# Reordering one block's up items and two sets of weight sums in a fused attention and FFN kernel

## The chip, the cores and the metric

The kernel runs on one core of one Trainium2 chip. The metric is the device time of one execution in microseconds (us), the median of several runs. The core has five engines with a queue of instructions each: TensorE (PE in the profile, PEld for its weight loads), VectorE (DVE), ScalarE (ACT), GpSimd (POOL) and SyncE (SP), which here issues most of the transfers. Each engine works through its own queue in order and waits where an operand or a buffer is not ready; the queues wait for each other by semaphores.

## The reference

```python
q_n = q / (np.linalg.norm(q, axis=-1, keepdims=True) + 1e-06)      # k_n, c_n alike
q_assign = np.argmax(np.einsum('bhsd,hcd->bhsc', q_n, c_n), axis=-1)   # k_assign alike
mask = q_assign[:, :, :, None] == k_assign[:, :, None, :]
scores = scale * np.matmul(q, k.transpose(0, 1, 3, 2))
scores = np.where(mask, scores, -1000000000.0)
...
attn = attn / (np.sum(attn, axis=-1, keepdims=True) + 1e-09)
...
x = np.ascontiguousarray(attn_out.transpose(0, 2, 1, 3)).reshape(B * S, H * D)
h = x @ w_in
relu6 = np.clip(h + 3.0, 0.0, 6.0)
g = h * relu6 / 6.0
return (g @ w_out).astype(np.float32)
```

Four batches of 768 tokens, 8 heads of 64: attention in which a query sees only keys of its own cluster (16 per head), then a feed-forward block of 512 to 2048 to 512 with hard-swish. Inputs are 64-bit floats; the kernel works in 32 bits.

## The kernel before

The work has three stages. A **loop** (`for n in range(0, total + lag_d + 2, 2)`, "round n" below) does attention for the first two batches: 8 pairs of heads, 12 steps a pair, two steps a round. Each round issues the scores and exponentials of its steps (L400, L423), GpSimd's running sums over the exponentials (L430, L433, `acc`), and the products with the values of the two steps before (`pv`, L443). Every sixth step the sums are added up on TensorE (`pd`, L467), inverted and multiplied on VectorE (`rcp` L473, `num` L474) and written to `xd`. Between these stands the preparation of the next pair, by the place r of the round in the pair: transposes of queries and keys (`pqk`, L320) at r = 0 and 2, cluster scores (`pcs`, L337) at r = 4, their transposes and one-hot rows on VectorE (`pr`, `mx` L351, `one_hot` L357) at r = 6, and the transposes of the one-hot rows (`po`, L379; copied by ScalarE to `xm`, L384) at r = 8 and 10.

The same loop decodes the weights from 64 bits, in 32 chunks of five steps, mostly on VectorE (L232 to L259), a number of steps a round set by `share`. Behind the chunks, `decode` holds eight weight sums (L523): halves of T1, T2, T4 and T3, differences of the four blocks of `w_out`, 128 x 1024 each.

From round 60 on the loop also takes items of the feed-forward block of the first batch. An **up item** (L597, 16 matmuls into one PSUM bank `ph`) multiplies 256 tokens by two slices of `w_in`; ScalarE lifts the result (L499), VectorE clips it (L502), and after every second item GpSimd makes four sums of gated values (L635). The eight up items of this first block are multiplied out plainly; all later blocks use `halved` (L645, `uX`, `uY`), a seven-product scheme that needs, for each slice i, three sums of blocks of `w_in` (t1, t2, t4) and a fourth that replaces block b12 in place. `make_first_sums(i)` makes them (L556) and stores the three in DRAM (`td`, L557), from where later blocks load them (`tx`, L548); the sums for i = 0 and 1 stay in SBUF for the second block. As b12 is overwritten, the fourth sum of slice i can come only after the first block's up item i.

Behind the up items stand seven **down parts** of the block (L684), each in two halves, which multiply the gated values by `w_out` or T1 to T4 into the banks `X` and `Y`; VectorE and ScalarE take the banks into `y` (L691, L735). The first block's parts run at the end of the loop and in the second stage. Part 3 reads T3, which takes the place of one block of `w_out`, parts 0 and 1 read T2, part 2 T1, part 6 T4. In the first block each part's `end` also calls `make_first_sums` for the slices listed for it, ahead of its own `y` sums.

In the loop nearly all PSUM results of one bank (`ph`, `pqk`, `pcs`, `pr`, `pd`, `po`, `X`, `Y`) share two banks (`psum_m`, `scratch`), so each waits until the one before the last is read.

The second stage (`late_plan`) does attention for the other two batches over tokens sorted by cluster, with GpSimd scattering rows through DRAM (L1014, from the positions `pos`), mixed with feed-forward items; the third finishes the feed-forward block.

The order of all queues is the order in which the program issues (`manual_schedule`). Before, `want` spreads the items evenly from round 60 on, and places each ahead of the preparation of the same round; the list is 60, 64, 70, 74, 80, 84, 90, 94 for the up items and 100 for the first down part. `share` leaves weight sum 0 to round 90, 1 to 3 to round 92 and 4 to 7 to round 94.

Of the kernel before, what the change touches and what calls it, by code (L numbers as in the profile page):

```python
# [119 lines left out]
def fast_path(ctx, tc, ok, q, k, v, centroids, moe_w_in, moe_w_out, out):  # L120
# [390 lines left out]
    def weight_sums(i):  # L511
        if i == 0:
            decoding.close()
            wtp = pool("wtp", 1)
            for name in ("T1", "T2", "T4"):
                st[name] = wtp.tile([P, HF, HC], F32, name=name)
            st["T3"] = wb[0][1]
        name, a, b = (
            ("T1", wb[0][1], wb[0][0]), ("T2", wb[1][1], st["T1"]), ("T4", wb[1][0], st.get("T2")),
            ("T3", wb[1][1], wb[0][1]),  # L520
        )[i // 2]
        h = slice(i % 2 * HF // 2, (i % 2 + 1) * HF // 2)
        nc.vector.tensor_tensor(out=st[name][:, h], in0=a[:, h], in1=b[:, h], op=ALU.subtract)  # L523
# [15 lines left out]
    def wi(s, t, i):  # L539
        f = t * HF + i  # L540
        return w_in_sb[:, s * HK : (s + 1) * HK, f * P : (f + 1) * P]
# [5 lines left out]
            tx = st["tx", u] = txp.tile([P, 3, HK, P], F32, name="tx")  # L547
            nc.sync.dma_start(tx, td[:, i])  # L548

    def make_first_sums(i):  # L550

        tx = txp.tile([P, 3, HK, P], F32, name="tx")
        t1, t2, t4 = (tx[:, k] for k in range(3))
        b11, b12, b21, b22 = wi(0, 0, i), wi(0, 1, i), wi(1, 0, i), wi(1, 1, i)
        for out_, in0, in1 in ((t1, b12, b11), (t2, b22, t1), (t4, b21, t2), (b12, b22, b12)):
            nc.vector.tensor_tensor(out=out_, in0=in0, in1=in1, op=ALU.subtract)  # L556
        nc.sync.dma_start(td[:, i], tx)  # L557
        if i < 2:
            st["tx", HF + i] = tx

    def token_sums(b, m):

# [15 lines left out]
    def ffn_items(b):  # L578
# [114 lines left out]
        def down(m, part):  # L693
            def keep(chunk, half, y, queue=nc.sync):
                queue.dma_start(out_v[b, 2 * m + chunk][:, half * HC : (half + 1) * HC], y)

            def multiply(second):
                if part < 2:
                    h = range(part * HF // 2, (part + 1) * HF // 2)
                    if second:  # L700
                        product(st["X"], 1, 5, st["T2"], False, True, False, h)
                    else:
                        product(st["X"], 0, 0, wb[0][0], True, False, False, h)
                    return
                kind, bank, half, w = (
                    (4, "Y", 0, st["T1"]), (1, "Y", 1, st["T3"]),
                    (2, "X", 0, wb[1][0]), (6, "Y", 0, wb[1][1]), (3, "Y", 1, st["T4"]),
                )[part - 2]
                h = range(second * HF // 2, (second + 1) * HF // 2)
                product(st[bank], half, kind, w, part == 2, part in (3, 4, 6), part > 3, h)  # L710

            def begin():
                raise_gates()
                if part == 0:
                    st["X"] = psum_m.tile([P, DM], F32, name="X", tag="m")
                    st["y0"] = yp.tile([P, DM], F32, name="y0", tag="y0")
                elif part == 2:
                    st["Y"] = st.get("psum_y", psum_m).tile([P, DM], F32, name="Y", tag="m")
                    st["y1"] = yp.tile([P, DM], F32, name="y1", tag="y1")
                multiply(0)  # L720

            def end():
                multiply(1)
                if part == 0:
                    finish()
                if (b, m, part) == (B - 1, NHC - 1, 6):
                    st["good"] = nc.values_load(ok[0:1, 0:1], min_val=0, max_val=1)
                if part == 4:
                    token_sums(*divmod(b * NHC + m + 1, NHC))
                if (b, m) == (0, 0):  # L730
                    for i in ([HF - 1, HF - 2], [5], [4], [], [3, 2], [0], [1])[part]:
                        make_first_sums(i)
                y0, y1 = st["y0"], st.get("y1")
                if part == 1:
                    nc.scalar.copy(out=y0[:, HC:], in_=st["X"][:, HC:])  # L735
                    add(y0[:, HC:], y0[:, HC:], st["X"][:, 0:HC])
                elif part == 3:
                    add(y1[:, 0:HC], y0[:, HC:], st["Y"][:, HC:])
                    add(y1[:, HC:], y1[:, 0:HC], st["Y"][:, 0:HC])
                    keep(1, 1, y1[:, HC:])  # L740
                elif part == 4:
                    nc.scalar.copy(out=y0[:, 0:HC], in_=st["X"][:, 0:HC])
                    keep(0, 0, y0[:, 0:HC])
                elif part == 6:
                    add(y1[:, 0:HC], y0[:, HC:], st["Y"][:, HC:])
                    keep(1, 0, y1[:, 0:HC])
                    add(y0[:, HC:], y0[:, HC:], st["Y"][:, 0:HC])

                    keep(0, 1, y0[:, HC:], nc.scalar if st["last"] else nc.sync)

            return [begin, end]

# [475 lines left out]
    per_batch = NKT * per_pair  # L1228
    total = FIRST * per_pair
    lag_v, lag_d = 2, 4  # L1230
    up_first = NFT // 2

    decode = [step for i in range(NW) for step in decoding_steps(i)]
    decode += [lambda i=i: weight_sums(i) for i in range(8)]
    READY, DECODED = per_batch + 2 * lag_d, 2 * per_batch

    def share(n, r):  # L1240


        if n < READY:
            return {0: 4, 2: 3, 4: 3, 6: 1, 8: 2, 10: 4}[r]
        if n < DECODED - per_pair:
            return {0: 6, 2: 5, 4: 4, 6: 3, 8: 5, 10: 5}[r]
        return {0: 6, 2: 5, 4: 4, 6: 1, 8: 3, 10: 4}[r]
# [2 lines left out]
    st["early"] = st["free"] = True  # L1250
    st["last"] = st["moving"] = False
    fill, checks = [], []
    st["done"] = 0

    def check_all():
        now, checks[:] = checks[:], []
# [7 lines left out]
    with tc.manual_schedule():  # L1264
        nc.scalar.dma_start(cen, centroids.rearrange("h c d -> (h c) d"))
        load(0, "q", "k")
        constants()
        load(0, "v")
        load_weights(0)
        centroid_norm()  # L1270
        for part in range(3):
            turn(0, part)
        idle(5)
        nc.vector.tensor_copy(out=ident_q, in_=ident)
        load(1, "q", "k")
        load_weights(1)
        cluster_scores(0)
        scores_qk(0)
        route(0)
        scores_qk(1)  # L1280
        for part in range(2):
            route_turn(0, part)

        for n in range(0, total + lag_d + 2, 2):
            g, r = divmod(n, per_pair)
            steps = [i for i in (n, n + 1) if i < total]
            prep = prep_items(g + 1, r)
            for i in steps:
                scores(i)
                exponentials(i)  # L1290
                key_sums(i)
            for i in (n - lag_v, n - lag_v + 1):
                if 0 <= i < total:
                    attn_v(i)
            m = n - lag_d + 1
            if m >= 0 and m % NCH == NCH - 1:
                later.append(divide(m))
                ready(m)
            if prep and r == 4:
                prep.pop(0)()  # L1300
            if r == 6:
                load(g + 2, "q", "k")
                load(g + 1, "v")
            want = min(max(n + 2 - READY, 0) * up_first // (DECODED - READY) - st["done"], len(fill) // 2)
            st["done"] += want
            for i in range(max(len(prep), want)):
                if i < want:
                    fill.pop(0)()
                    fill.pop(0)()
                if i < len(prep):  # L1310
                    prep[i]()
            if n < total:
                for step in decode[: share(n, r)]:
                    step()
                del decode[: share(n, r)]
            check_all()
            checks.extend(later)
            later.clear()

        while checks or later:  # L1320
            checks.extend(later)
            later.clear()
            check_all()
        st["early"] = False
        st["moving"] = True
        open_late()
        for i, point in enumerate(late_plan()):
            for op, *args in point:
                op(*args)
            busy = i >= AHEAD and (i - AHEAD) % SLOT in (6, 9)  # L1330
            if fill and not busy:
                fill.pop(0)()
        st["last"] = True
        st["moving"] = False
        flag = whether_good()
        while fill:
            fill.pop(0)()
            if len(fill) == HOLD:
                flag()
# [363 lines left out]
```

## Time and profile before

| | us |
|---|---|
| median of 3 runs | 957.33 (957.01 to 957.46) |
| the profiled execution | 959.56 |
| its span, first to last instruction | 957.8 |
| TensorE's granted clock | 0.998 |

The profile is one execution. Its page lists busy time by engine, the span in 40 slices, and groups of instructions by line, engine and operands. A row of the timeline has the start and the length in us, the engine, the line, the operation, and operands with shapes; "x16" means that so many instructions follow each other. In square brackets stands how long the engine stood idle before it, and what it then waited for. A row of waits has the sum, the number and the longest. A row of a stretch ("windows") has its bounds, its length, and the busy time of PE, PEld, DVE, ACT and POOL with the number of instructions, then TensorE's granted clock, the DMA engines' busy share and GB/s.

### The profile page before, as it was taken

To read this page: it belongs to the slowest core of one execution; us is meant where nothing else is said; L and a number is where in the kernel's file an instruction comes from. 1 tells how busy PE (TensorE), PEld (TensorE's weight loads), DVE (VectorE), ACT (ScalarE), POOL (GpSimd) and SP (SyncE) were. 2 spreads that over 40 slices of the span, in tenths; PEclk is the share of its full clock that TensorE was granted. 3 is DMA by queue.
4 is the path that set the end of the run, shared out by engine and by line. 5 is a ranking of instruction groups with operands and counts; after the bars stand their busy time and mean duration, and the time that the engine had idled before them with its cause. 6 is when DMAs were issued, how large, how long until landed. Compare 5 with 4: busy or idle time off the path is not lost.

```text
span 957.8 us, 17621 instructions
## 1 busy us (share of the span) xinstructions
PE 929.6 (97%) x6358; PEld 725.5 (76%) x6358; DVE 594.4 (62%) x1306; ACT 349.8 (37%) x731; POOL 576.3 (60%) x1302
## 2 busy tenths in 40 slices
PE   8999999999899999999999999999999999999997
PEld 5444445555698798787897988888888799999996
DVE  6789888989977276274483474374471564636261
ACT  6888877765112232222232231241331311202020
POOL 3877767657367577776777878767777160303030
PEclk9999999999999999999999999999999999999999
DMA  7255464350474557456584484654744333323210
GB/s 206 90 133 155 132 176 124 106 145 10 145 223 137 151 159 164 129 130 153 153 198 119 120 204 118 160 155 114 198 142 95 102 96 116 102 72 105 66 57 26
DMA packets 174351, 124.23 MB, mean 130 GB/s; under 512 B 134064, under 2 KB 152496, under 8 KB 174256
## 3 DMA queue, kind: packets, MB, share of 16 engines
q1 hardware_dynamic: 164320, 109.86, 42.7%
q0 software_dynamic: 9216, 12.60, 4.4%
q8 instruction: 52, 0.85, 0.4%
q10 hardware_dynamic: 720, 0.56, 0.2%
q14 instruction: 43, 0.35, 0.1%
HBM read 94.67 MB, written 28.31 MB: 128 GB/s over the span
## 4 chain that ended last, share of the span: by engine, by line
PE 67%; DVE 3%; DMA 2%; issue 1%; ACT 0%; SPq 0%; another core or an unknown queue 0%; ACTq 0%; DVEq 0%
PE Y L684 17%; PE uY L645 15%; PE X L684 12%; PE uX L645 11%; PE pv L1096 3%; PE ps L899 3%; PE ps L1057 3%; DMA piece<-qd 2%; PE pv L1057 1%; PE pd L1120 1%; PE pcs L337 1%; PE rk L981 1%; PE ps L1137 1%; DVE tx L556 0%; DVE w_out_sb L523 0%
## 5 line engine op out<-in xcount | busy, mean ns | idle before, releaser
L433 POOL TENSOR_TENSOR acc<-acc,ex 128x768 f32<-128x768 f32 x64 | 123.3, 1927 | 37.4 <-ACT ex L423 33.9
L1014 POOL DMA_INDIRECT qd<-qn,pos x96 | 96.2, 1002 | 54.8 <-issue 17.5
L1030 POOL DMA_INDIRECT xn<-xsd,pos x96 | 94.3, 982 | 46.0 <-ACT sx L499 24.3
L499 ACT ACTIVATE sx<-g_sb,half_c 128x512 f32<-128x512 f32 x88 | 63.8, 725 | 146.5 <-DVE g_sb L656 126.3
L635 POOL TENSOR_TENSOR g_sb<-g_sb 128x256 f32<-128x256 f32 x52 | 41.8, 825 | 122.1 <-DVE g_sb L502 121.1
L1014 POOL DMA_INDIRECT kvd<-kvn,pos x96 | 96.1, 1001 | 27.3 <-issue 25.4
L1006 POOL MEMSET w_low<- 128x1 f32 x864 | 91.3, 106 | 33.3
L691 DVE TENSOR_TENSOR y<-y,Y 128x256 f32<-128x256 f32 x48 | 20.2, 421 | 132.7 <-PE Y L684 131.9
L684 PE MATMUL X<-w_out_sb,g_sb 128*128 128x256 f32 x384 | 90.4, 382 | 4.0 <-DVE y L691 2.2
L645 PE MATMUL uX<-xb,w_in_sb 128*128 128x128 f32 x704 | 93.0, 275 | 0.0
L684 PE MATMUL Y<-T,g_sb 128*128 128x256 f32 x384 | 88.0, 381 | 0.0
L684 PE MATMUL Y<-w_out_sb,g_sb 128*128 128x256 f32 x384 | 87.7, 380 | 0.0
L645 PEld LDWEIGHTS uX<-xb,w_in_sb 128*128 128x128 f32 x704 | 85.7, 192 | 0.0
L684 PEld LDWEIGHTS X<-w_out_sb,g_sb 128*128 128x128 f32 x384 | 70.9, 190 | 18.5 <-issue 4.0
L684 PEld LDWEIGHTS Y<-T,g_sb 128*128 128x128 f32 x384 | 72.1, 190 | 13.2 <-issue 3.9
L684 PEld LDWEIGHTS Y<-w_out_sb,g_sb 128*128 128x128 f32 x384 | 71.9, 190 | 10.6 <-issue 1.3
L656 DVE TENSOR_TENSOR sx<-uX,sx 128x128 f32<-128x128 f32 x176 | 51.1, 290 | 45.9 <-ACT sx L663 30.8
L400 PE MATMUL ps<-xf 64*128 64x384 f32 x384 | 78.5, 487 | 0.6 <-ACT ex L423 0.6
L423 ACT ACTIVATE ex<-ps 128x768 f32<-128x768 f32 x96 | 72.6, 802 | 4.5 <-PE ps L400 4.5
L443 PE MATMUL pv<-ex,vt 128*64 128x384 f32 x384 | 72.5, 499 | 0.0
L502 DVE SCALAR_TENSOR_TENSOR g_sb<-sx,g_sb 128x512 f32<-128x512 f32 x88 | 63.9, 728 | 3.3 <-ACT sx L499 2.3
L656 DVE TENSOR_TENSOR g_sb<-uY,sx 128x128 f32<-128x128 f32 (+1 forms) x176 | 65.6, 414 | 0.0
(194 smaller groups left out, 1796.7 us busy)
## 6 DMA issues: line engine op xcount, KB each, us to landing
tx<-td SPq DMA_DIRECT2D x86, 384.0 KB
raw<-in_moe_w_in_dram SPq DMA_DIRECT2D x16, 512.0 KB
raw<-in_moe_w_out_dram SPq DMA_DIRECT2D x16, 512.0 KB
xb<-xd SPq DMA_DIRECT2D x12, 512.0 KB
out_dram<-y SPq DMA_DIRECT2D x44, 128.0 KB
qk<-in_q_dram SPq DMA_DIRECT2D x18, 192.0 KB
qk<-in_k_dram SPq DMA_DIRECT2D x18, 192.0 KB
vt<-in_v_dram SPq DMA_DIRECT2D x16, 192.0 KB
```

The costliest lines, as they stand in the source:

```text
L400: nc.tensor.matmul(st["ps", n][:, t, 0:HALF], lhsT=x[r, NCH + j], rhs=x[r, hf * NHC : (hf + 1) * NHC], start=first, stop=last, skip_group_ ...
L423: nc.scalar.activation(out=ex, in_=sc, func=ACT.Exp, scale=SM_SCALE)
L433: nc.gpsimd.tensor_tensor(out=acc, in0=acc, in1=ex, op=ALU.add)
L443: nc.tensor.matmul(pv[t * D : (t + 1) * D], lhsT=vt[:, t, j], rhs=ex[:, t], start=(j == 0), stop=(j == NCH - 1),)
L499: nc.scalar.activation(out=r, in_=h, func=ACT.Relu, bias=half_c, scale=1.0 / 6.0)
L502: nc.vector.scalar_tensor_tensor(out=g, in0=r, scalar=1.0, in1=h, op0=ALU.min, op1=ALU.mult)
L645: nc.tensor.matmul(dst, lhsT=w[:, kt], rhs=x(kt), start=(kt == 0), stop=(kt == HK - 1))
L656: nc.vector.tensor_tensor(out=out_, in0=in0, in1=in1, op=ALU.add)
L684: nc.tensor.matmul(bank[:, half * HC : (half + 1) * HC], lhsT=g_sb[:, kind, i], rhs=w[:, i], start=(first and i == 0), stop=(last and i == ...
L1006: nc.gpsimd.memset(w_low, W_LOW)
L1014: i = nc.gpsimd.indirect_dma_start(out=rows[name, g, t], in_=src, in_offset=None, out_offset=bass.IndirectOffsetOnAxis(ap=pos[:, a, j, t : ...
L1030: nc.gpsimd.indirect_dma_start(out=xn[:, j, t], out_offset=None, in_=rows["xsd", g, t], in_offset=bass.IndirectOffsetOnAxis(ap=pos[:, 0, j ...
```

## The change

The up items and the first down part get a list of rounds, `up_at`, and are taken after the preparation of the round. `make_first_sums` is split: `kept_sums(i)` makes t1, t2, t4 and stores them, the in-place subtraction remains. For the slices 7, 6, 5, 4 `kept_sums` runs in the loop at rounds 64, 70, 76 and 82, behind the decoding steps; for the others where it stood. The last four weight sums (T4 and T3) leave `decode` and are issued with down parts 0 to 3, T3 first. The sums of a down part now come after its `y` sums.

```diff
+    def subtract(out_, in0, in1):
+        nc.vector.tensor_tensor(out=out_, in0=in0, in1=in1, op=ALU.subtract)
+
+    def kept_sums(i):
         tx = txp.tile([P, 3, HK, P], F32, name="tx")
         t1, t2, t4 = (tx[:, k] for k in range(3))
-        b11, b12, b21, b22 = wi(0, 0, i), wi(0, 1, i), wi(1, 0, i), wi(1, 1, i)
-        for out_, in0, in1 in ((t1, b12, b11), (t2, b22, t1), (t4, b21, t2), (b12, b22, b12)):
-            nc.vector.tensor_tensor(out=out_, in0=in0, in1=in1, op=ALU.subtract)
+        for sums in ((t1, wi(0, 1, i), wi(0, 0, i)), (t2, wi(1, 1, i), t1), (t4, wi(1, 0, i), t2)):
+            subtract(*sums)
         nc.sync.dma_start(td[:, i], tx)
         if i < 2:
             st["tx", HF + i] = tx
+        st["kept"].add(i)
+
+    def make_first_sums(i):
+        if i not in st["kept"]:
+            kept_sums(i)
+        subtract(wi(0, 1, i), wi(1, 1, i), wi(0, 1, i))
...
                 if part == 4:
                     token_sums(*divmod(b * NHC + m + 1, NHC))
-                if (b, m) == (0, 0):
-                    for i in ([HF - 1, HF - 2], [5], [4], [], [3, 2], [0], [1])[part]:
-                        make_first_sums(i)
                 y0, y1 = st["y0"], st.get("y1")
...
                     keep(0, 1, y0[:, HC:], nc.scalar if st["last"] else nc.sync)
+                if (b, m) == (0, 0):
+                    for i in ([HF - 1, HF - 2], [5], [4], [], [3, 2], [0], [1])[part]:
+                        make_first_sums(i)
+                    if part in (0, 1):
+                        weight_sums(6 + part)
+                    elif part in (2, 3):
+                        weight_sums(2 + part)
...
-    up_first = NFT // 2
...
-    decode += [lambda i=i: weight_sums(i) for i in range(8)]
+    decode += [lambda i=i: weight_sums(i) for i in range(4)]
+    st["kept"] = set()
+    kept_at = {64: 7, 70: 6, 76: 5, 82: 4}
+    up_at = (58, 64, 70, 76, 82, 88, 94, 96, 100)
...
-            want = min(max(n + 2 - READY, 0) * up_first // (DECODED - READY) - st["done"], len(fill) // 2)
-            st["done"] += want
-            for i in range(max(len(prep), want)):
-                if i < want:
-                    fill.pop(0)()
-                    fill.pop(0)()
-                if i < len(prep):
-                    prep[i]()
+            for step in prep:
+                step()
+            if n in up_at:
+                fill.pop(0)()
+                fill.pop(0)()
             if n < total:
                 for step in decode[: share(n, r)]:
                     step()
                 del decode[: share(n, r)]
+                if n in kept_at:
+                    kept_sums(kept_at[n])
```

More of the change, by code (lines that the diff above doesn't have):

```diff
@@ L548, in first_sums @@
             nc.sync.dma_start(tx, td[:, i])
-    def make_first_sums(i):
+    def subtract(out_, in0, in1):
+        nc.vector.tensor_tensor(out=out_, in0=in0, in1=in1, op=ALU.subtract)
+    def kept_sums(i):
         tx = txp.tile([P, 3, HK, P], F32, name="tx")
         t1, t2, t4 = (tx[:, k] for k in range(3))
-        b11, b12, b21, b22 = wi(0, 0, i), wi(0, 1, i), wi(1, 0, i), wi(1, 1, i)
-        for out_, in0, in1 in ((t1, b12, b11), (t2, b22, t1), (t4, b21, t2), (b12, b22, b12)):
-            nc.vector.tensor_tensor(out=out_, in0=in0, in1=in1, op=ALU.subtract)
+        for sums in ((t1, wi(0, 1, i), wi(0, 0, i)), (t2, wi(1, 1, i), t1), (t4, wi(1, 0, i), t2)):
+            subtract(*sums)
         nc.sync.dma_start(td[:, i], tx)
@@ L1252, in fast_path @@
     fill, checks = [], []
-    st["done"] = 0
     def check_all():
```

## The prediction

> **What bounds the kernel now.** I read the totals of the page first, then TensorE's waits, then both queues in order of time over the stretch that the change touches.
>
> ```profile
> span 957.8 us, 17621 instructions
> PE 929.6 (97%) x6358; PEld 725.5 (76%) x6358; DVE 594.4 (62%) x1306; ACT 349.8 (37%) x731; POOL 576.3 (60%) x1302
> ...
> PE X L684 <- DVE y L691: 2.2, 1, 2.2
> PE X L684 <- DVE g_sb L502: 1.8, 1, 1.8
> ```
>
> TensorE is busy for 97% of the span, so the change can win only gaps of TensorE, 28 us in all. The two named waits lie in the stage of the change. In order of time they, and the gaps ahead of them, are:
>
> ```profile
> 132.50 0.92 PE L400 MATMUL ps<-xf 64*128 64x384 f32 x4 [0.33 <-ACT ex L423]
> 133.91 0.50 PE L400 MATMUL ps<-xm 64*128 64x384 bf16 x4 [0.49 <-ACT xm L384]
> ...
> 141.39 0.66 PE L320 MATMUL pqk<-ident,qk 128*128 128x128 f32 x4 [0.82 <-ACT xf L326]
> ...
> 169.23 0.50 PE L379 MATMUL po<-ident_q,one_hot 128*128 128x128 bf16 x6
> 169.66 0.92 PE L400 MATMUL ps<-xf 64*128 64x384 f32 x4
> ...
> 240.09 0.81 PE L467 MATMUL pd<-acc,ones 128*64 128x384 f32 x4
> 242.73 1.99 PE L684 MATMUL X<-w_out_sb,g_sb 128*128 128x256 f32 x8 [1.82 <-DVE g_sb L502]
> ...
> 253.19 3.62 PE L684 MATMUL Y<-w_out_sb,g_sb 128*128 128x256 f32 x16
> 259.02 1.99 PE L684 MATMUL X<-w_out_sb,g_sb 128*128 128x256 f32 x8 [2.21 <-DVE y L691]
> ...
> 270.12 0.61 PE L645 MATMUL uX<-xs,tx 128*128 128x128 f32 x4
> ```
>
> VectorE's queue says what sets the two large gaps. An up item's clip (L502) is the place where VectorE itself waits:
>
> ```profile
> 140.90 0.69 DVE L502 SCALAR_TENSOR_TENSOR g_sb<-g_sb,ph 128x512 f32<-128x512 f32 x1 [2.30 <-ACT g_sb L499]
> 154.80 0.69 DVE L502 SCALAR_TENSOR_TENSOR g_sb<-g_sb,ph 128x512 f32<-128x512 f32 x1 [2.15 <-ACT g_sb L499]
> 170.15 0.69 DVE L502 SCALAR_TENSOR_TENSOR g_sb<-g_sb,ph 128x512 f32<-128x512 f32 x1 [1.18 <-ACT g_sb L499]
> ...
> 211.57 0.69 DVE L502 SCALAR_TENSOR_TENSOR g_sb<-g_sb,ph 128x512 f32<-128x512 f32 x1 [3.31 <-ACT g_sb L499]
> ...
> 228.63 0.69 DVE L502 SCALAR_TENSOR_TENSOR g_sb<-g_sb,ph 128x512 f32<-128x512 f32 x1 [0.51 <-ACT g_sb L499]
> 230.29 2.78 DVE L523 TENSOR_TENSOR T<-w_out_sb 128x1024 f32<-128x1024 f32 x1
> 232.99 2.54 DVE L473 RECIPROCAL rcp<-pd 128x384 f32<-128x384 f32 x1
> 235.57 1.48 DVE L474 TENSOR_TENSOR num<-num,rcp 128x384 f32<-128x384 f32 x1
> 239.72 2.35 DVE L523 TENSOR_TENSOR T<-w_out_sb,T 128x1024 f32<-128x1024 f32 x2
> 241.99 0.68 DVE L502 SCALAR_TENSOR_TENSOR g_sb<-g_sb,ph 128x512 f32<-128x512 f32 x1
> 242.59 2.88 DVE L523 TENSOR_TENSOR T<-w_out_sb,T 128x1024 f32<-128x1024 f32 x2
> 245.39 3.41 DVE L523 TENSOR_TENSOR w_out_sb<-w_out_sb 128x1024 f32<-128x1024 f32 x2
> 258.55 0.41 DVE L691 TENSOR_TENSOR y<-y,X 128x256 f32<-128x256 f32 x1
> ```
>
> From 170.15 on VectorE never rests except at the clips of 211.57 (3.31) and 228.63 (0.51). TensorE waits for VectorE at 242.73 (the first X takes the PSUM bank that the last clip frees) and at 256.81 (the next X product must wait for the y sum of 258.55, which stands behind T4, T3, a reciprocal and the first tx). So from 170 to 258 VectorE is the bound; behind 270 it is TensorE again. The sum therefore follows VectorE up to the first X, and TensorE behind it.
>
> **The change, part by part.** I write X for the first X product (242.73) and take the end of the second weight sums T2 (242.0) as the hinge.
>
> Up items moved. Before, their matmuls stood at 60, 64, 70, 74, 80, 84, 90, 94 of the loop; now at 58, 64, 70, 76, 82, 88, 94, 96, and always behind the one-hot rows (po) or cluster scores (pcs) of their round. The item at 58 fills TensorE while ScalarE makes xm and frees the score banks: the gaps of 0.33, 0.49 and 0.82 close, 1.64. Against it, at round 70 po (169.23 to 169.66, 0.43) now comes ahead of the item, so the clip comes that much later, and the lift of an item stands in ScalarE's queue ahead of the next exponentials; that wait I estimate at 0.4, about half the 0.82 just won. The clip of 170.15 comes 0.8 sooner. The item at 58 starts 4.2 us before the old one and needs its tokens by 132.2:
>
> ```profile
> 127.19 0.53 SPq L537 DMA_DIRECT2D xb<-xd  x1
> 131.00:132.00 1.00, 1.00 (x12) 0.40 (x8) 1.00 (x2) 0.97 (x5) 0.00 (x0) 1.00 1.05 366
> 132.00:133.00 1.00, 0.67 (x8) 0.30 (x4) 0.93 (x3) 1.00 (x2) 0.41 (x1) 1.00 0.38 144
> ```
>
> The first row is SP's issue of that load, the others are two stretches of 1 us, with the busy share of the DMA engines next to last. The transfers end at about 132.4 (share 1.05, then 0.38), and the last load in it is a raw weight behind xb: a wait of 0 to 0.2, taken as 0.
>
> Later items stand behind the reciprocal whose bank they take, so TensorE will wait for VectorE more often from 74 to 92. While VectorE is the bound that costs nothing of its own. It also means that VectorE no longer waits at 211.57 and 228.63: 3.8 won.
>
> One clip less lies ahead of T2 (items 6 and 7 are both clipped behind it): 0.6 won there, 0.6 paid back between T2 and X.
>
> Kept sums. Twelve subtractions (three for each of items 7, 6, 5, 4) move from the down stage into the loop. Their length:
>
> ```profile
> L556 DVE TENSOR_TENSOR tx<-w_in_sb,tx 128x256 f32<-128x256 f32 x16 | 6.9, 429 | 0.5
> ```
>
> The first group (round 64) falls into the stretch before 170.15, where VectorE waits 1.18 at the next clip: covered; without that cover it costs 1.3. The other nine lie where VectorE is the bound: 9 x 0.43 = 3.9 lost. That is their length with GpSimd at rest. In the loop it is not, as GpSimd's queue in order of time and two stretches of 24 us show:
>
> ```profile
> 174.89 1.81 POOL L430 TENSOR_TENSOR acc<-ex 128x768 f32<-128x768 f32 x1 [4.53 <-ACT ex L423]
> ...
> 230.18 4.57 POOL L433 TENSOR_TENSOR acc<-acc,ex 128x768 f32<-128x768 f32 x2 [3.33 <-ACT ex L423]
> ...
> 242.75 6.64 POOL L635 TENSOR_TENSOR g_sb<-g_sb 128x256 f32<-128x256 f32 x4 [4.03 <-DVE g_sb L502]
> ...
> 168.00:192.00 24.00, 22.95 (x146) 12.25 (x146) 22.07 (x27) 19.04 (x42) 15.56 (x12) 1.00 0.33 109
> 192.00:216.00 24.00, 22.01 (x132) 12.54 (x130) 20.02 (x26) 16.29 (x38) 13.78 (x10) 1.00 0.48 139
> ```
>
> The same weight sum takes 2.35 / 2 = 1.17 at 239.72, with GpSimd idle, and 2.78 at 230.29, where a GpSimd sum of 1.81 had begun at 230.18: it waited that out. T4 and T3 against GpSimd's four gated sums took turns, both slower. So a subtraction of two SBUF operands that meets a GpSimd sum waits for its end, and the next may wait again. GpSimd (fifth busy column) is at work 15.56 + 13.78 of 48 us, 0.61. First of a group: 0.61 x 1.81 / 2 = 0.55. The other two: GpSimd has its next sum ready perhaps 0.4 of the time, 0.72 each. A group 2.0, three groups 6.0. The bounds: 0 (all in GpSimd's pauses, of which 4.53 before 174.89 is the nearest), and half a sum plus two whole ones each time, 3 x 4.5 = 13.6. I take 6.0, the row of 230.29 being nearest in kind.
>
> The Trainium skill, "SBUF — State Buffer", section "Who interferes with whom", has the same as an exclusive lock: a VectorE instruction with two SBUF inputs against a GpSimd one that reads SBUF, whoever comes first holding it to the end. The trace agrees (2.78 against 1.17). By it the moved sums cost about the 6.0 above; were the port shared out instead, they would cost some 2.
>
> X starts at 242.0 - 0.8 - 3.8 - 0.6 + 3.9 + 6.0 = 246.7 (end of T2), and from there two clips and the 0.74 that lies between 241.99 and 242.73: 246.7 + 0.6 + 0.7 = 248.0, that is 5.3 late.
>
> Down stage. T3 and T4 move behind the y sum, the final b12 subtractions stay, and the y sums now stand ahead of the tx work of their part. Behind the last clip VectorE has 2.5 (reciprocal), 0.6 to 1.5 (num), two subtractions 0.9, half of T3 1.2 and about 2 of small work before the y sum: done some 8 after X, and TensorE asks 256.81 - 242.73 = 14.1 after it. The wait of 2.21 goes. T3's second half is done about 10 after X; the product that reads it starts 10.5 after (253.19), its second half 1.7 later. T4 is asked last. From X to the first uX TensorE then needs 27.4 - 2.2 = 25.2 without a stop. Only four of the eight tx groups are left there, so the positions, which release GpSimd's scatters, are ready as long ahead of uX as before, and the later stages shift as a whole. The four td stores go out in the loop, each one issue on SP behind the raw loads, which run two chunks ahead: 0; without that cover about a third of a microsecond each.
>
> Net: 5.3 - 2.2 = +3.1. The profiled execution took 959.56 with 1.8 around its span of 957.8, so it would take 962.7; against the median of the runs shown, 957.33, that is **960.4**.
>
> **Rivals.** About 0.2%, 1.9 us, is what a measurement of this kernel can tell from no change.
>
> (1) Faster: the nine sums fall into GpSimd's pauses. For it: GpSimd rests 39% of the time and VectorE waited 9 us at the five clips quoted; the group of round 70 would stand just ahead of 174.89. Against it: three groups directly follow ends of rounds, when the next exponentials arrive. Then 3.1 - 6.0 = -2.9, 954.4.
>
> (2) The waits are about half, 1.2 to 5.0: gain and loss cancel, 957.3 give or take 1.9.
>
> (3) T3 becomes the wait. If GpSimd's gated sums hold VectorE's SBUF work behind the clip for more than the 2 us of lead, the Y product at 253.19 stops; their own length, half of 6.64, bounds it at 1.3: 961.7.
>
> (4) The change does not do what it says: the y sum still comes too late and the 2.21 stays: 962.6. Against it the lead of 6 us.
>
> **How the numbers follow.** Forecast (waits of about 6) 0.42; (1) 0.26; (2) 0.20; (3) 0.06; (4) 0.06. Slower by over 0.2%: 0.54, same 0.20, faster 0.26. The range goes from rival (1), 954.3, to waits of 10, 3.1 + 4.0 = +7.1, 964.4. The forecast's own range is 959.2 to 963.
>
> **What would show it.** Right: the kept subtractions in the loop at well over 0.43 each or followed by it, VectorE's clips without idle time from 170 on, the up items waiting for L473's reciprocal, first X at about 248, no wait for y behind it, 25.2 from X to uX. Wrong: tx rows at 0.43 in the loop and X before 243; or a gap between X and uX; or a uX shift that does not reach the end, for instance taken up in TensorE's wait for the ranked pieces.

## The result and the profile after

| | us |
|---|---|
| changed kernel, median of 6 runs | 962.56 (961.6 to 967.85) |
| before, 6 runs beside it | 957.17 (954.24 to 957.94) |
| ratio | 1.0074, 95% interval [1.0046, 1.0102] |
| the profiled execution (its span) | 967.85 (966.1) |

Slower by 0.74%. The ratio is that of the means of the six runs; the medians lie 5.4 apart, 0.56%. The forecast was 960.4. The profiled execution is the slowest of the six, so a second profile of the same kernel was taken later (`k_again` below); what is read here holds in both unless it is said. From the page of the changed kernel, and its list of TensorE's waits (sum, times, longest):

```profile
span 966.1 us, 17626 instructions
PE 935.6 (97%) x6358; PEld 730.9 (76%) x6358; DVE 603.6 (62%) x1306; ACT 349.5 (36%) x731; POOL 576.6 (60%) x1302
...
PE po L379 <- DVE one_hot L357: 6.8, 3, 3.9
...
PE ph L605 <- DVE rcp L473: 3.9, 2, 2.4
PE ph L605 <- DVE wunit L248: 2.1, 1, 2.1
```

Of the two waits of before, the one for `y` (2.2) is off the list and the one for the clip is down from 1.8 to 0.7. In their place TensorE waits for VectorE's one-hot rows and reciprocals, inside the loop. TensorE is also busy 6.0 longer with the same 6358 instructions (935.6 against 929.6), at a granted clock of 0.989 instead of 0.998. The same in order of time, TensorE's rows with the largest gaps:

```profile
134.64 5.38 PE L605 MATMUL ph<-xb,w_in_sb 128*128 128x256 f32 x16 [2.05 <-DVE wunit L248]
...
167.00 0.82 PE L379 MATMUL po<-ident_q,one_hot 128*128 128x128 bf16 x6 [2.59 <-DVE one_hot L357]
...
190.66 3.72 PE L605 MATMUL ph<-xb,w_in_sb 128*128 128x256 f32 x16 [1.53 <-DVE rcp L473]
...
205.73 0.82 PE L379 MATMUL po<-ident_q,one_hot 128*128 128x128 bf16 x6 [3.90 <-DVE one_hot L357]
...
231.45 5.41 PE L605 MATMUL ph<-xb,w_in_sb 128*128 128x256 f32 x16 [2.40 <-DVE rcp L473]
...
257.71 1.99 PE L692 MATMUL X<-w_out_sb,g_sb 128*128 128x256 f32 x8 [0.70 <-DVE g_sb L502]
...
282.62 0.61 PE L653 MATMUL uX<-xs,tx 128*128 128x128 f32 x4
```

The same 16 products of an up item take 3.72 in one place and 5.38 and 5.41 in two others. The first X product starts 15.0 after its place in before (257.71 against 242.73), the first uX 12.5 (282.62 against 270.12).

What VectorE did ahead of the late one-hot rows are the kept subtractions. VectorE's rows at the four rounds:

```profile
160.97 0.94 DVE L551 TENSOR_TENSOR tx<-w_in_sb 128x256 f32<-128x256 f32 x1
161.94 3.88 DVE L551 TENSOR_TENSOR tx<-w_in_sb,tx 128x256 f32<-128x256 f32 x2
166.32 0.62 DVE L357 TENSOR_TENSOR one_hot<-pr,mx 128x192 bf16<-128x192 f32 x2
...
180.96 2.03 DVE L551 TENSOR_TENSOR tx<-w_in_sb 128x256 f32<-128x256 f32 x1
183.02 0.89 DVE L551 TENSOR_TENSOR tx<-w_in_sb,tx 128x256 f32<-128x256 f32 x2
...
199.69 0.97 DVE L551 TENSOR_TENSOR tx<-w_in_sb 128x256 f32<-128x256 f32 x1
200.69 3.86 DVE L551 TENSOR_TENSOR tx<-w_in_sb,tx 128x256 f32<-128x256 f32 x2
205.05 0.62 DVE L357 TENSOR_TENSOR one_hot<-pr,mx 128x192 bf16<-128x192 f32 x2
...
220.75 0.41 DVE L551 TENSOR_TENSOR tx<-w_in_sb 128x256 f32<-128x256 f32 x1
221.20 2.38 DVE L551 TENSOR_TENSOR tx<-w_in_sb,tx 128x256 f32<-128x256 f32 x2
```

and GpSimd's at the first of them:

```profile
158.27 3.36 POOL L643 TENSOR_TENSOR g_sb<-g_sb 128x256 f32<-128x256 f32 x4 [1.95 <-DVE g_sb L502]
161.59 2.00 POOL L430 TENSOR_TENSOR acc<-ex 128x768 f32<-128x768 f32 x1
163.67 3.81 POOL L433 TENSOR_TENSOR acc<-acc,ex 128x768 f32<-128x768 f32 x2
```

Alone, a group of three takes 1.3 (0.41 + 0.88). Here the four take 4.8, 2.9, 4.8 and 2.8. At round 64 GpSimd has three kinds of sums ready without a pause from 158.27 to 167.5, and the subtractions end at 161.9, 163.9 and 165.8: about one for each GpSimd sum. The groups of rounds 64 and 76 follow a clip that releases the four gated sums (L643); those of rounds 70 and 82 follow one that releases none, and are the short ones. The second profile differs in one of them: its groups take 4.8, 1.3, 4.8 and 2.9, so that of round 70 met no GpSimd sum:

```profile
179.56 0.42 DVE L551 TENSOR_TENSOR tx<-w_in_sb 128x256 f32<-128x256 f32 x1
180.01 0.89 DVE L551 TENSOR_TENSOR tx<-w_in_sb,tx 128x256 f32<-128x256 f32 x2
```

### The profile page after: what moved, and what is told of

It reads as the page before. It is cut to its first block, busy times and chain, and to the rows that moved or that the text cites. A ratio compares the mean times of both kernels' runs of the same rounds, so it can differ in the third digit from the quotient of the medians.

```text
span 966.1 us, 17626 instructions
## 1 busy us (share of the span) xinstructions
PE 935.6 (97%) x6358; PEld 730.9 (76%) x6358; DVE 603.6 (62%) x1306; ACT 349.5 (36%) x731; POOL 576.6 (60%) x1302
## 4 chain that ended last, share of the span: by engine, by line
PE 86%; DVE 7%; DMA 3%; ACT 2%; issue 1%; POOL 0%; SPq 0%; DVEq 0%; ACTq 0%; POOLq 0%
PE Y L692 17%; PE uY L653 15%; PE X L692 13%; PE uX L653 11%; PE ps L400 6%; PE pv L443 5%; PE pv L1108 3%; PE ps L911 3%; PE ph L605 3%; PE ps L1069 3%; DMA piece<-qd 2%; DVE tx L551 2%; PE pv L1069 1%; PE pqk L320 1%; PE pcs L337 1%
## 5 line engine op out<-in xcount | busy, mean ns | idle before, releaser
L643 POOL TENSOR_TENSOR g_sb<-g_sb 128x256 f32<-128x256 f32 x52 | 38.1, 756 | 128.3 <-DVE g_sb L502 127.3
L400 PE MATMUL ps<-xf 64*128 64x384 f32 x384 | 80.9, 500 | 0.0
```

Source lines behind the costliest of these rows:

```text
L400: nc.tensor.matmul(st["ps", n][:, t, 0:HALF], lhsT=x[r, NCH + j], rhs=x[r, hf * NHC : (hf + 1) * NHC], start=first, stop=last, skip_group_ ...
```

## The experiments

Theory K, the first theory throughout: the kept sums in the loop carry the loss, by VectorE's turns with GpSimd. The rivals: the second theory of the first four runs, that the new places of the up items carry it; theory F, that the early first item does; and L, that the mere length of twelve more instructions is enough. All ratios are to the kernel before on the same chip, with 95% intervals; the last two columns are from each kernel's profile.

| kernel | median us | ratio | first X | first uX |
|---|---|---|---|---|
| before | 957.33 | | 242.73 | 270.12 |
| changed | 962.56 | 1.0074 [1.0046, 1.0102] | 257.71 | 282.62 |
| a_no_kept | 952.34 | 0.9946 [0.9927, 0.9966] | 238.94 | 264.47 |
| b_kept_only | 961.45 | 1.0043 [1.0030, 1.0056] | 250.16 | 275.07 |
| c_up_only | 955.05 | 0.9971 [0.9959, 0.9984] | 241.81 | 269.34 |
| d_down_only | 956.43 | 0.9986 [0.9975, 0.9998] | 242.91 | 268.80 |
| e_first_60 | 966.52 | 1.0099 [1.0082, 1.0116] | 253.68 | 278.59 |
| f_one_psum | 954.81 | 0.9975 [0.9965, 0.9986] | 243.88 | 268.79 |
| g_pauses | 957.13 | 1.0003 [0.9991, 1.0015] | 244.89 | 269.80 |
| h_no_kept_60 | 952.11 | 0.9950 [0.9936, 0.9963] | 240.21 | 265.75 |
| i_two_58 | 954.85 | 0.9951 [0.9935, 0.9967] | 240.83 | 265.75 |
| j_only_64 | 958.33 | 0.9988 [0.9973, 1.0002] | 243.69 | 268.60 |
| k_again | 967.51 | 1.0072 [1.0047, 1.0097] | 253.81 | 278.72 |

The kernel before ran at 957.5 beside a to d, at 957.4 beside e to h, and at 960.5 on the chip of i to k; so these last are read by their ratios.

**The parts, one at a time.** The changed kernel without kept sums in the loop, then each part alone on the kernel before.

```diff
-    kept_at = {64: 7, 70: 6, 76: 5, 82: 4}
+    kept_at = {}
```

> The changed kernel, but the four groups of kept sums stay in the down stage. Theory 1 (the kept sums in the loop, each held up by GpSimd's sums, carry the loss): the 15.2 us that the twelve subtractions take in the loop of the changed kernel's trace go, the waits of 2.6 and 3.9 for one_hot go, and the time falls to 954 to 956, below the kernel before. Theory 2 (the up items' places carry it: the first item's wait of 2.05 at round 58, the waits of 1.5 and 2.4 for the reciprocal, the halved clock behind them): it stays at 960 to 963.

b_kept_only is the kernel before with `kept_sums` split off and called in the loop as in the change:

```diff
+                if n in kept_at:
+                    kept_sums(kept_at[n])
```

> The kernel before with the kept sums in the loop and nothing else: up items and weight sums as before, sums ahead of the y sums in the down parts. Theory 1: 960 to 963, about the whole loss, less the wait of 2.2 ahead of X that should shrink since three groups leave the down parts 0 and 1. Theory 2: 955 to 958.

c_up_only is the kernel before with the new places alone:

```diff
-            want = ...
+            for step in prep:
+                step()
+            if n in up_at:
+                fill.pop(0)()
+                fill.pop(0)()
```

> The kernel before with the new places of the up items and nothing else. Theory 1: 955 to 958; the prediction has 0.8 won up to round 70. Theory 2: 960 to 963, with TensorE's wait of about 2 at the first item and its matmuls at half clock.

d_down_only is the kernel before with the order of the down stage alone (T3 and T4 with the parts, the sums behind `y`):

```diff
-    decode += [lambda i=i: weight_sums(i) for i in range(8)]
+    decode += [lambda i=i: weight_sums(i) for i in range(4)]
...
+                    if part in (0, 1):
+                        weight_sums(6 + part)
+                    elif part in (2, 3):
+                        weight_sums(2 + part)
```

> The kernel before with the down stage alone changed: T3 and T4 issued with the down parts, all sums behind the y sums, no kept sums in the loop. Both theories: the wait of 2.2 ahead of the second X product goes and nothing else, 954.5 to 955.5. If the later stages take the gain up, 957.

The kept sums are the only part that makes the kernel slower, alone (1.0043) and with the rest (0.9946 without them, 1.0074 with them). The other two win: 0.29% and 0.14% alone, 0.54% together (0.34 to 0.73), which this noise does not tell from the sum of the two. Two forecasts were missed: a_no_kept came out below its 954 to 956 (952.34), d_down_only above its 954.5 to 955.5 (956.43). In c_up_only TensorE's row at the first X shows what the down stage adds, beside the same row and T3's in a_no_kept:

```profile
241.81 3.78 PE L684 MATMUL X<-w_out_sb,g_sb 128*128 128x256 f32 x8 [4.00 <-DVE g_sb L502]
```

```profile
238.94 1.99 PE L692 MATMUL X<-w_out_sb,g_sb 128*128 128x256 f32 x8 [0.70 <-DVE g_sb L502]
...
251.64 1.99 PE L692 MATMUL Y<-w_out_sb,g_sb 128*128 128x256 f32 x8 [0.35 <-DVE w_out_sb L523]
```

With the new places alone T4 and T3 still stand ahead of the last clip in VectorE's queue, and the items' gain ends in a wait of 4.00 there, behind which eight products take 3.78 instead of 1.99. Moved behind the `y` sums, they leave 0.70, and T3 itself is late by 0.35.

**The first item.** The changed kernel, and the one without kept sums, with the first item at round 60.

```diff
-    up_at = (58, 64, 70, 76, 82, 88, 94, 96, 100)
+    up_at = (60, 64, 70, 76, 82, 88, 94, 96, 100)
```

> The changed kernel with the first up item at round 60 instead of 58; the kept sums stay. Theory K (the kept sums in the loop carry the loss, by their length and by the turns that VectorE takes with GpSimd): the wait of about 2 for the tokens ahead of the first item goes, and with it the stretch at half clock behind it (16 products in 5.38 instead of 3.72), but the first clip comes some 4 later, so that the kept group of round 64 has less of VectorE's idle time ahead of it. Net between -2 and 0 against the changed kernel: 960.5 to 962.5, still slower than before. Theory F (the early first item, with its wait for the tokens, makes the loss): 957.5 or less.

> The changed kernel without kept sums in the loop (all eight groups in the down stage) and the first item at round 60. Without the kept sums the wait for the tokens ahead of the first item is 1.1 and the clock stays up, so theory K gives 951.3 to 953.3, no difference from the same kernel with the first item at 58 (952.3) within 1. Theory F: 950 or less.

Without kept sums the place makes no difference (0.9950 against 0.9946). With them the kernel did not become faster, as K had expected by up to 2, and F by 5: 966.52 lies above both forecasts, at a ratio of 1.0099, whose interval overlaps that of the changed kernel. VectorE's rows in e_first_60, clips and the first kept group:

```profile
143.74 0.69 DVE L502 SCALAR_TENSOR_TENSOR g_sb<-g_sb,ph 128x512 f32<-128x512 f32 x1 [4.75 <-ACT g_sb L499]
156.14 0.69 DVE L502 SCALAR_TENSOR_TENSOR g_sb<-g_sb,ph 128x512 f32<-128x512 f32 x1
159.60 0.95 DVE L551 TENSOR_TENSOR tx<-w_in_sb 128x256 f32<-128x256 f32 x1
160.58 3.88 DVE L551 TENSOR_TENSOR tx<-w_in_sb,tx 128x256 f32<-128x256 f32 x2
...
233.76 0.68 DVE L502 SCALAR_TENSOR_TENSOR g_sb<-g_sb,ph 128x512 f32<-128x512 f32 x1
```

The group of round 64 still takes 4.8, and the wait for one-hot rows stays at 3.9. F falls; the early item and its wait for tokens are not the loss. Up to the first X nothing is gained or lost (253.68, and 253.81 in the second profile of the changed kernel); why the median is above what K allowed is open.

**Turns or length.** In f_one_psum each kept subtraction of the loop has a PSUM tile as its first operand instead of an SBUF slice, so the true second weights of slices 7 to 4 are left out; number, size and place are those of the change (`early` is set for the calls in the loop).

```diff
+            if early:
+                in0 = st["top"][:, 0 : HK * P].bitcast(F32).rearrange("p (k c) -> p k c", k=HK)
             subtract(out_, in0, in1)
```

> In the loop each of the twelve kept subtractions takes a PSUM tile as its first operand instead of an SBUF slice: same number, size and output tiles, but the sums of items 7 to 4 are not the true ones, so the second weights of these slices are left out. Theory K in the form of turns (a subtraction of two SBUF operands waits for a GpSimd sum to end): with one SBUF operand a group takes its length alone, about 1.3 to 1.5 instead of 2.75 to 4.8, in all some 9 to 10 of VectorE less, and TensorE's waits of 2.6 and 3.9 for one-hot rows fall below 1.5: 954 to 957. Rival L (the mere length and place of twelve more instructions, GpSimd not involved): groups and time as in the changed kernel, 961 to 963.

```profile
159.43 0.41 DVE L551 TENSOR_TENSOR tx<-wtop,w_in_sb 128x256 f32<-128x256 f32 x1
159.87 0.88 DVE L551 TENSOR_TENSOR tx<-wtop,tx 128x256 f32<-128x256 f32 x2
161.26 0.62 DVE L357 TENSOR_TENSOR one_hot<-pr,mx 128x192 bf16<-128x192 f32 x2
```

```profile
156.72 3.37 POOL L645 TENSOR_TENSOR g_sb<-g_sb 128x256 f32<-128x256 f32 x4 [1.95 <-DVE g_sb L502]
160.05 1.83 POOL L430 TENSOR_TENSOR acc<-ex 128x768 f32<-128x768 f32 x1
```

These are VectorE's rows of round 64, then GpSimd's. The same GpSimd sums run beside the group, and the group takes 1.3 instead of 4.8; so do the other three, and the kernel falls from 1.0074 to 0.9975. That is K in the form of turns: 0.99% of 1.28% that the kept sums cost in all (1.0074 less 0.9946), and 0.29% for the rest, which is their length and what the shift of everything behind them brings. The Trainium skill, "SBUF — State Buffer", section "Who interferes with whom", has it that a VectorE instruction with at most one SBUF input, outside its two-port modes, stays out of GpSimd's way; the trace agrees, 0.42 a subtraction beside the running sums of 160.05.

In g_pauses the sums are true and stand where GpSimd rests:

```diff
-    kept_at = {64: 7, 70: 6, 76: 5, 82: 4}
+    kept_at = {58: (7, 6), 70: (5,), 82: (4,)}
...
+            if n == 58:
+                for i in kept_at[n]:
+                    kept_sums(i)
             if n in up_at:
                 fill.pop(0)()
                 fill.pop(0)()
+            if n in kept_at and n != 58:
+                for i in kept_at[n]:
+                    kept_sums(i)
...
-                if n in kept_at:
-                    kept_sums(kept_at[n])
```

> The same twelve kept sums, all true, at other places of the loop: two groups at round 58 ahead of the item, one each at rounds 70 and 82 directly behind the item's clip and ahead of the decoding, where GpSimd pauses (4.89 and 6.43 idle ahead of its sums of 180.89 and 220.83). Theory K in the form of turns: groups near their length of 1.3, 952.5 to 956, that is between the kernel without kept sums (952.3) and that plus 12 x 0.43 less what VectorE's idle time covers. Rival L (length alone): the cost is as in the changed kernel wherever they stand, 960 to 963.

```profile
134.86 2.04 DVE L551 TENSOR_TENSOR tx<-w_in_sb 128x256 f32<-128x256 f32 x1
136.94 0.88 DVE L551 TENSOR_TENSOR tx<-w_in_sb,tx 128x256 f32<-128x256 f32 x2
...
171.90 0.42 DVE L551 TENSOR_TENSOR tx<-w_in_sb 128x256 f32<-128x256 f32 x1
172.36 0.88 DVE L551 TENSOR_TENSOR tx<-w_in_sb,tx 128x256 f32<-128x256 f32 x2
```

One subtraction of twelve met a GpSimd sum (2.04), the others took 0.42 to 0.44. The time is no longer to be told from before (1.0003), though it lies above the 952.5 to 956 that K expected: two groups at rounds 70 and 82 still push VectorE where it is the bound, and `ph` waits 2.40 for a reciprocal at 220.31. L, which had 960 to 963, falls. The two groups are 2.6 long, yet the first X is 4.1 later than in i_two_58, which lacks them (244.89 against 240.83). The eight multiplications behind the reciprocals (`num`, L474, two SBUF operands) say where more of it went: they take 8.5 here and 6.0 there, because they now meet GpSimd's sums more often.

**Which groups are free.** i_two_58 is g_pauses with only the two groups at round 58, j_only_64 the changed kernel with only that of round 64.

```diff
-    kept_at = {58: (7, 6), 70: (5,), 82: (4,)}
+    kept_at = {58: (7, 6)}
```

> The changed kernel with only two kept groups in the loop, both at round 58 ahead of the first item's clip; the other six groups are made in the down stage. Theory K (a group costs only what VectorE's idle time does not cover): VectorE waits 2.80 at that clip in the kernel without kept sums, the two groups took 4.2 there (2.04 + 0.88 + 0.42 + 0.88), so 1.4 are left, and the down stage is 2.6 shorter: 951.5 to 953.5. Rival L (each kept group in the loop costs its share of the 10, wherever it stands): 956 to 958.

```diff
-    kept_at = {64: 7, 70: 6, 76: 5, 82: 4}
+    kept_at = {64: 7}
```

> The changed kernel with only the kept group of round 64 in the loop, the one that was predicted as covered by VectorE's wait at the next clip. If it is covered, as predicted: 952.3, as without kept sums. Theory K with the turns counted: the group takes 4.8 instead of 1.3, VectorE's idle time at the next clip is 1.5, and the one-hot rows that TensorE waits for stand behind it: wait of about 2 for one_hot at 163 to 167, 954 to 956.

The two at round 58 cost nothing that can be measured in time (0.9951 against 0.9946), though the first X is 1.9 later than in a_no_kept: there VectorE waits 2.80 for its clip anyway. The one at round 64 costs 0.42% (0.9988 less 0.9946), some 4.0, though its interval is wide. VectorE's rows of j_only_64, then TensorE's:

```profile
158.22 0.94 DVE L551 TENSOR_TENSOR tx<-w_in_sb 128x256 f32<-128x256 f32 x1
159.20 3.88 DVE L551 TENSOR_TENSOR tx<-w_in_sb,tx 128x256 f32<-128x256 f32 x2
...
175.17 0.68 DVE L502 SCALAR_TENSOR_TENSOR g_sb<-g_sb,ph 128x512 f32<-128x512 f32 x1
```

```profile
164.25 0.51 PE L379 MATMUL po<-ident_q,one_hot 128*128 128x128 bf16 x6 [2.62 <-DVE one_hot L357]
```

It takes 4.8 again, TensorE waits 2.62 for the one-hot rows behind it, and VectorE's idle time at the next clip (1.48 without kept sums) is used up. So some of the group is covered, and still the first X is 4.75 later than in a_no_kept (243.69 against 238.94). The rows of `num` behind the group, in a_no_kept and then in j_only_64 with GpSimd's sums, show what takes the cover back:

```profile
164.80 0.56 DVE L474 TENSOR_TENSOR num<-num,rcp 128x384 f32<-128x384 f32 x1
```

```profile
168.80 2.06 DVE L474 TENSOR_TENSOR num<-num,rcp 128x384 f32<-128x384 f32 x1
168.63 3.90 POOL L433 TENSOR_TENSOR acc<-acc,ex 128x768 f32<-128x768 f32 x2 [3.89 <-ACT ex L423]
```

TensorE's wait makes the exponentials later, GpSimd's sums, which wait for them, start 2.3 later than in a_no_kept (168.63 against 166.36), and `num` now meets one and takes 1.5 longer.

**The changed kernel again**, unaltered.

> The changed kernel itself, for a second profile of it and more times on the same chip as the others: 961.5 to 963.5. If its profile is a run of the middle, TensorE's waits for one_hot and rcp stand as in the first profile, with fewer stretches at half clock: clock 0.993 to 0.996 against 0.989, first X at about 252 instead of 257.7.

```profile
164.54 0.51 PE L379 MATMUL po<-ident_q,one_hot 128*128 128x128 bf16 x6 [2.59 <-DVE one_hot L357]
...
202.73 0.51 PE L379 MATMUL po<-ident_q,one_hot 128*128 128x128 bf16 x6 [3.90 <-DVE one_hot L357]
...
227.55 5.41 PE L605 MATMUL ph<-xb,w_in_sb 128*128 128x256 f32 x16 [2.40 <-DVE rcp L473]
...
253.81 1.99 PE L692 MATMUL X<-w_out_sb,g_sb 128*128 128x256 f32 x8 [0.70 <-DVE g_sb L502]
```

The same waits for one-hot rows, the same ratio (1.0072), and the first X at 253.81, nearer the expected 252 than the 257.71 of the first profile. The median, 967.51, lies above the expected 961.5 to 963.5, on a chip on which before takes 3 more as well. The first profile's 3.9 more at the first X belong to that execution: it lost the clock in four stretches of the loop, this one in two.

## Why the prediction was right, and where it was not

The time, 962.56, lies in the range of 954.3 to 964.4 and in the forecast's own 959.2 to 963 (by the ratio of the means it is 964.4, the range's end), and the mechanism (turns of the kept sums with GpSimd) is the one that f and g show. By its steps:

- **Up items.** The clip of 170.15 was to come 0.8 sooner; in a_no_kept it stands at 170.35. What failed here is the tokens' wait, taken as 0 to 0.2: it was 1.1 there and 1.5 in the second profile of the changed kernel. (The first has 2.05 at that place, but names VectorE's `wunit` as the last to come.) Most of the 3.8 of VectorE's idle time at the later clips did go: a_no_kept has 0.41 left, at 218.84. Without all kept sums the working gives the first X at 248.0 - 9.9 = 238.1; a_no_kept has 238.94. That it comes so near is in part luck: T2 ends at 236.46 there, reckoned at 246.7 - 9.9 = 236.8, although the clip of round 70 came 1.0 later than reckoned, and VectorE is idle for 1.14 ahead of the last clip, which the working did not have.
- **Nine kept sums.** 3.9 of length and 6.0 of turns, 9.9. The rows of the last three groups give 2.9 + 4.8 + 2.8 = 10.5 in the first profile and 1.3 + 4.8 + 2.9 = 9.0 in the second, and the first X moves by 253.81 - 243.69 = 10.1 from j_only_64 to the second profile. This was right in sum, with some luck: the turns were not 2.0 a group but 3.5 behind gated sums and 0 to 1.6 elsewhere, and the working leaves out that VectorE's other work meets other GpSimd sums once it is shifted. The eight `num` take 6.1 in a_no_kept, 8.3 in j_only_64 and 10.0 in the second profile (6.2 in the first, so this too changes from one execution to the next).
- **The first group** is the step that failed: "covered: without that cover it costs 1.3". It takes 4.8 in each kernel that has it with two SBUF operands, and it moved the first X by 4.75. Turns were counted for the other nine sums and not for these three, though four gated sums of GpSimd stand directly beside them, and the one-hot rows that TensorE asks for next stand behind them. The cover itself was there (1.48 at the next clip in a_no_kept), but the later `num` took about as much again. The first X was forecast at 248.0; with 4.75 more, 252.75, against 253.81 in the second profile. The time would have been 960.4 + 4.75 = 965.2; the ratio gives 957.33 x 1.0074 = 964.4 (961.7 to 967.1).
- **Down stage.** Right. The 2.21 is gone, and from X to uX TensorE needs 24.9 in both profiles (282.62 - 257.71), forecast 25.2.
- **Later stages shift as a whole.** In the table the shift of the first uX and the shift of the time (ratio less 1, times 957.3) agree within 2.0 for a to k: -5.7 and -5.2 for a, +4.9 and +4.1 for b, +8.6 and +6.9 for k, c the farthest with -0.8 and -2.8. The first profile alone stands off, +12.5 against +8.3 of its own time. The two profiles of one kernel need 683.5 and 689.5 from uX to the end, on two chips, so a few us there are the execution's or the chip's. Both seem to play a part: the other two kernels on the chip of the second need 687.3 and 686.1, those of a to h 683.4 to 685.9, and the second profile lost the clock once more there, behind a wait of 2.08 that ends at 625.53.
- **Rivals.** Sums in GpSimd's pauses, the faster rival, happen where the change puts them only for the group of round 70 in the second profile, the very one the rival named (in b_kept_only, where the up items stand elsewhere, those of rounds 70 and 76 take 1.3 too); put there, as most are in g, they bring the kernel back to 1.0003. T3 as a wait shows only without the kept sums, 0.3 to 0.7 (a_no_kept, d_down_only, h_no_kept_60). That the wait of 2.21 stays fell.

The versions that beat both kernels by most are the change without its kept sums in the loop (0.9946 [0.9927, 0.9966]; the same with the first item at 60) and the one with two groups at round 58. They can't be told apart. c_up_only (0.9971) and d_down_only (0.9986) beat both by less.

## What to carry to other kernels

Before VectorE work with two SBUF operands is moved into a loop, look at GpSimd's queue at that very place, and price each instruction at one GpSimd instruction more where that queue has no pause; a mean busy share hides how much the places differ, here 4.8 a group at two of them and 1.3 to 2.9 at the others. Idle time of the engine behind a moved step is a safe cover only if no instruction that another engine asks for stands between the two: here the late one-hot rows shifted GpSimd's sums onto other work of VectorE. And try the parts of a change one by one: here two of three won 0.54% together, and the third turned that into a loss of 0.74%.

## What was not expected of the hardware

TensorE's clock. In the first profile four stretches of the loop, in the second two, run at a granted clock of 0.50, each beginning in a wait or shortly behind one. Stretches of 2 us of the second (clock third from the end):

```profile
200.00:202.00 2.00, 0.00 (x0) 0.00 (x0) 2.00 (x2) 0.00 (x0) 1.92 (x2) 1.00 0.00 0
202.00:204.00 2.00, 1.27 (x12) 0.80 (x14) 1.93 (x5) 0.73 (x2) 1.21 (x1) 0.94 0.80 286
204.00:206.00 2.00, 2.00 (x10) 0.72 (x6) 1.97 (x2) 1.94 (x8) 0.00 (x0) 0.50 1.03 230
206.00:208.00 2.00, 2.00 (x11) 0.64 (x10) 1.91 (x2) 1.81 (x4) 0.75 (x1) 0.71 1.22 235
```

Behind the wait of 3.90 that ends at 202.7 the clock stays up for about a microsecond and is then at 0.50 until some time in 206 to 208. All waits of 3.3 to 4.0 in the loop were followed by it (both profiles of the changed kernel, b, c, e). Shorter ones were or were not: 2.59 and 2.40 were in the first profile, but 2.59 was not in the second, nor 2.40 in g (its item takes 3.72), nor 2.21 in before; 2.17 was in e and was not in b. In the second stage TensorE waits 2.03 to 2.25 for a `piece` somewhere between 609 and 626 in nearly every kernel, before among them (2.14); c, d, e, j and the second profile lost the clock behind it, before, a, b, f, g, h and i did not. An up item that falls into it takes 1.7 longer (5.41 less 3.72). The Trainium skill, "TensorE: Matmul & The Clock Gate", section "Part 1: The HAM clock gate (the "warmup" mystery)", lets the clock fall after an idle window of about 3.4 us, with windows that run freely. That the same wait sometimes costs and sometimes doesn't agrees with free windows; that waits of 2.05 and 2.40 were enough does not agree with a whole idle window. So a new wait of over 2 us can have a second price, here 1.7 for an up item and 2.6 for the first sixteen X products of c_up_only (6.2 instead of 3.6), which the prediction did not have. How much of the 0.99% is the clock's was not measured by itself. The clock is not the whole loss of the change: one run of k_again had a mean granted clock of 1.0 and took 964.53, and before, on the same chip, took 956.17 to 960.07 in its three runs at 0.999.
